# One bank per role: how five PSUM banks are handed out in the key/value stage of a linear-attention layer

## The chip, the cores and the metric

The kernel runs on one core of a Trainium2 chip. Its time is the device time in microseconds (us) of one execution, and the figure to compare is the median over several runs. The core has five engines with instruction streams of their own that run side by side and wait for each other through semaphores: TensorE (PE in the profile: matmuls, with weight loads shown as PEld), VectorE (DVE), ScalarE (ACT), GpSimd (POOL) and SyncE (SP), which starts the DMAs. Each engine executes its stream in order. Matmul results land in PSUM, which is divided into eight banks; a bank holds one 128 x 512 tile of f32. The other engines read the results from there.

## The reference, cut to what matters

The input x has 2048 rows of 1024. Four layers follow each other: attention, feed-forward, attention, feed-forward, with the same weights for both attention layers and for both feed-forward layers. Each adds to x.

```python
def _A_ref(x, wqkv, wo):          # x: layernorm of the running x
    qkv = (x @ wqkv) ...          # q, k, v: 32 heads of 32
    phi = lambda t: where(t > 0, t + 1, exp(t)) + 1e-6
    pq, pk = phi(q), phi(k)
    kv = einsum("bhsd,bhse->bhde", pk, v)
    z = einsum("bhsd->bhd", pk)
    num = einsum("bhqd,bhde->bhqe", pq, kv)
    den = einsum("bhqd,bhd->bhq", pq, z) + 1e-6
    return (num / den) ... @ wo

def _B_ref(x, w_gate, w_up, w_down):
    return ((x @ w_gate) * (x @ w_up)) @ w_down
```

The part that matters here is in the second attention layer: k = x @ wk and v = x @ wv for all 2048 rows, phi(k), and the sums kv and z over the rows.

## The kernel before, in words

The order of all work is written out by hand: the program emits the instructions engine by engine in the order in which the Python code runs, and the framework adds the semaphore waits that the data and the reuse of buffers need. Three queues hand out buffers, first in, first out (class `Free`): `slots` (SBUF, 8 KB a partition), `temps` (SBUF tiles of 128 x 512 f32) and `banks` (the eight PSUM banks). `get` takes the one that was returned longest ago; `put` returns one. A bank may be returned in the program while its last reader has yet to run: the next matmul that writes it then gets a wait for that reader.

The second attention layer computes k and v with a scheme of seven block products in place of eight (`kv_seven`). The contraction of 1024 is split in two halves, and so are the rows and the columns; sums and differences of blocks of x and of the weights are made ahead on VectorE (`x_sum`, `w_sum`). The stage has eight units (`unit(u)`). A unit makes k and v of two tiles of 128 rows, in 14 steps given by `SEQ` (L519). A step is one block product: four matmuls of 128 x 128 by 512 columns (L582), and then whatever the other engines do with the result. Step "6v" is product 6 for v.

Three of the eight banks hold the running sums kv and z (`kvp`) through the stage, so exactly five are left, and a unit uses five, in these roles:

- "ak" and "av": products 1, 6, 7 and 4 of k and of v, added onto each other;
- "ck" and "cv": products 5 and 3 of k and of v;
- "b": product 2, first of k, then of v. For k, ScalarE copies product 1 into it (L587) and 2k is added on top.

On its way the unit runs: ScalarE copies of partial results to SBUF (L558, L592), VectorE adds that bring a partial result and a bank together (L561, L566), the exponential of phi (L287) and its two VectorE passes (L291, L293). Work that is to be emitted a step or more later is put into `plan` by `later`: `out4` (L569), a ScalarE copy that reads the result of 4v out of "av", is emitted two steps after 4v, which is behind step 1k of the next unit. Behind 3k comes the exponential of a tile of 128 x 1024 (the "wide" one), its two VectorE passes one step later, and behind 3v the VectorE add L561 that reads "cv". After its steps a unit runs `kp` for the rows of the unit before it: 16 small matmuls (L527) that add into `kvp`.

The same plan holds work of other kinds: the layer norm of the rows of the second half (L234, L237, L242, L243, L245, L251, L258, L260, L262), their transposes by DMA (L274), the sums of x blocks (L218), loads of weights, and on GpSimd the cast of the query weights (L183).

A bank is taken when its role first occurs in a unit and returned when the program has emitted its last reader. In the order of the steps the roles take banks as ak and b (at 1k), ck (5k), av (1v), cv (5v). They return them as ak (4k), b (2v), ck (3k), cv (3v), and av last, since `out4` is emitted in the next unit. In the next unit the queue therefore gives ak, b and ck the banks that had the same role, gives av (at 1v) the bank of the old cv, and gives cv (at 5v) the bank of the old av.

The layer before ends with a product whose four banks are read by four VectorE instructions (L1167) and returned in that order; the stage's five banks are the last ones in the queue then. After the stage the queue goes on with the query projection (`q_step`, L791), which takes banks from it one by one.

Of the kernel before, what the change touches and what calls it, by code (L numbers as in the profile page):

```python
# [35 lines left out]
def kernel(  # L36
# [47 lines left out]
    banks = Free([psum.tile([P, NB], F32, tag=f"b{i}", name=f"b{i}") for i in range(8)])  # L84

    def v3(s, n):
        return s[:].rearrange("p (k n) -> p k n", n=n)
# [7 lines left out]
    def load_cols(view, n, parts=1):  # L95
        s = slots.get()
        w = KD // parts
        for r in range(parts):
            nc.sync.dma_start(out=v3(s, NB)[:, r * w:(r + 1) * w, :],
                              in_=view[:, r * w:(r + 1) * w, n * NB:(n + 1) * NB])  # L100
        return s
# [101 lines left out]
    def w_rhs(which, i):  # L203
        a11, a12, s4, a22, c, s3 = w_blocks(which)
        return {1: a11, 2: a12, 3: s4, 4: a22, 5: c[:, 0:KH], 6: c[:, KH:KD], 7: s3}[i]

    def x_blocks(g):
        x = h3(xnTs[(2, g)], NB)
        t = h3(xgs[g], 2 * P).rearrange("p (s k) n -> p s k n", k=KH)
        return x[:, 0:KH, 0:2 * P], x[:, KH:KD, 0:2 * P], x[:, 0:KH, 2 * P:NB], x[:, KH:KD, 2 * P:NB], t  # L210
# [73 lines left out]
    def phi_exp(b, c):  # L284
        m = temps.get()
        e = m[:].bitcast(BF16)[:, 0:b.shape[-1]]
        nc.scalar.activation(out=e, in_=b, func=ACT.Exp, bias=lns2[:, c:c + 1], scale=kaps[:, c:c + 1])  # L287
        return m, e
# [202 lines left out]
    def kv_seven(kvp):  # L491
        plan = {}

        def at(step, f, *args):
            plan.setdefault(step, []).append((f, args))

        for t, i in zip(range(2 * TPG, NT), (3, 8, 17, 31, 36, 45, 59, 64)):
            at(i, ln_stats, 2, t, (0,))
            if i % 14 == 8:
                at(i + 5, ln_norm, 2, t)  # L500
                at(i + 6, tr_tile, 2, t)
            else:
                at(i + 4, ln_rstd, 2, t)
                at(i + 6, ln_apply, 2, t)
                at(i + 7, tr_tile, 2, t)
        at(66, lambda: temps.put(st8.pop()))
        for g, i in ((1, 19), (2, 45), (3, 75)):
            for j in range(4):
                at(i + 2 * j, x_sum, g, j)
        at(8, load_w, "q", 0)  # L510
        at(9, load_w, "q", 1)
        for n in range(DC):
            for i in range(4):
                at(20 + 16 * n + 4 * i, cast_q, n, i)
        at(90, lambda: wA.update(o=[load_cols(wo_v, 0)]))

        pks = slots.get()
        pkv = v3(pks, D)
        SEQ = "1k 5k 1v 6k 2k 6v 7k 5v 7v 4k 2v 3k 4v 3v"  # L519
        wides = slots.get()  # L520
        wide = wides[:].bitcast(F32).rearrange("p (u n) -> p u n", n=D)

        def kp(t, first, last):
            u = t // TPG * 2 + t % 2
            r = 2 * (u % 2) + t % TPG // 2
            for c in range(KD):
                nc.tensor.matmul(out=kvp[c // 3][:, (c % 3) * VW:(c % 3) * VW + VW],  # L527
                                 lhsT=pkv[:, r, c * P:(c + 1) * P], rhs=vbs[r][:, c, :],
                                 start=first and c % 3 == 0, stop=last, skip_group_check=True)

        def tiles(u):
            return u // 2 * TPG + u % 2, u // 2 * TPG + u % 2 + 2

        def unit(u):
            g, pr = divmod(u, 2)
            b11, b21, b12, b22, t = x_blocks(g)
            lhs = {1: b11, 2: b21, 3: b22, 4: t[:, 3], 5: t[:, 0], 6: t[:, 1], 7: t[:, 2]}
            bk = {}
            tm = {}
            r0 = 2 * (u % 2)  # L540

            def pk(i, n):
                return pkv[:, r0 + i, n * NB:(n + 1) * NB]

            def vb(i, n):
                return vbs[r0 + i][:, n * (NB // P):(n + 1) * (NB // P), 0:P]

            def w4(a):
                return a[:].rearrange("p (c f) -> p c f", f=P)

            wd2 = wide[:, u % 2]

            def later(n, f, *args):
                at(u * 14 + j + n, f, *args)

            def copy(key, b):
                tm[key] = temps.get()
                nc.scalar.copy(out=tm[key][:], in_=b[:])  # L558

            def add(out, key, b):  # L560
                nc.vector.tensor_tensor(out=out, in0=w4(tm[key]), in1=w4(b), op=ALU.add)  # L561
                temps.put(tm.pop(key))

            def addw(n, b):
                v = wd2[:, n * NB:(n + 1) * NB]
                nc.vector.tensor_tensor(out=v, in0=v, in1=b[:], op=ALU.add)  # L566

            def out4(b):
                nc.scalar.copy(out=vb(0, 1), in_=w4(b))  # L569
                banks.put(b)  # L570

            for j, step in enumerate(SEQ.split()):
                i, w = int(step[0]), step[1]
                key = "b" if i == 2 else ("c" if i in (3, 5) else "a") + w
                if key not in bk:
                    bk[key] = banks.get()
                if i == 1 and w == "k":
                    bk["b"] = banks.get()
                b = bk[key]
                rhs = w_rhs(w, i)  # L580
                for k in range(KH):
                    nc.tensor.matmul(out=b[:], lhsT=lhs[i][:, k, pr * P:(pr + 1) * P], rhs=rhs[:, k, :],  # L582
                                     start=k == 0 and (i in (1, 5) or i == 2 and w == "v"), stop=k == KH - 1,
                                     skip_group_check=True)
                if i == 1:
                    if w == "k":
                        nc.scalar.copy(out=bk["b"][:], in_=b[:])  # L587
                    else:
                        copy("1v", b)
                elif i in (6, 7) and w == "k":  # L590
                    n = i - 6
                    nc.scalar.copy(out=wd2[:, n * NB:(n + 1) * NB], in_=b[:])  # L592
                    if i == 7:
                        later(1, addw, 1, bk["ck"])
                elif i == 6:
                    copy("6v", b)
                elif i == 7:
                    copy("7v", b)
                    add(vb(1, 1), "7v", bk["cv"])
                elif i == 3:  # L600
                    if w == "k":
                        addw(0, b)
                        later(1, phi_end, wd2, pkv[:, r0 + 1, :], 0, *phi_exp(wd2, 0))
                    else:
                        add(vb(1, 0), "6v", b)
                    banks.put(bk.pop(key))
                elif i == 2:
                    if w == "k":
                        phi_end(b[:], pk(0, 0), 0, *phi_exp(b[:], 0))
                    else:  # L610
                        add(vb(0, 0), "1v", b)
                        banks.put(bk.pop("b"))
                elif i == 4:
                    if w == "k":
                        phi_end(b[:], pk(0, 1), 0, *phi_exp(b[:], 0))
                        banks.put(bk.pop(key))
                    else:
                        later(2, out4, bk.pop(key))
                for f, args in plan.pop(u * 14 + j, ()):
                    f(*args)  # L620

        for u in range(2 * NG):
            unit(u)
            if u > 0:
                for t in tiles(u - 1):
                    kp(t, u == 1 and t == 0, False)
            if u % 2 == 1:
                slots.put(xgs.pop(u // 2))

        for i in sorted(plan):  # L630
            for f, args in plan[i]:
                f(*args)
        slots.put(*wA.pop("k"), *wA.pop("v"), wS.pop("k"), wS.pop("v"), wS.pop("d"), wides)
        wA["o"].append(load_cols(wo_v, 1))

        def rest():
            for t in tiles(2 * NG - 1):
                kp(t, False, t == NT - 1)
            slots.put(pks)
        return rest  # L640
# [92 lines left out]
    def layer_A(li, ahead):  # L733
        kvp = [banks.get() for _ in range(3)]
        rest = kv_eight(li, kvp) if li == 0 else kv_seven(kvp)

        kvx = slots.get()
# [551 lines left out]
```

## Time and profile before

| | us |
|---|---|
| median of 3 runs | 1510.17 |
| lowest and highest run | 1508.72 and 1510.45 |
| the profiled execution | 1509.88 |
| its span, first to last instruction | 1508.1 |
| the stage: first and last start of L582 | 757.7 and 872.9 |

The profile is one execution. Times in it are us from the start of its span. A timeline row gives the start, the duration, the engine and line, the operation with what it writes and reads and the shapes, and in brackets the idle time of the engine before it with the instruction that ended the wait. Rows of one line that follow each other are merged ("x8" is eight instructions). A matmul of 512 columns is shown with 379 ns, but matmuls overlap: they start about 216 ns apart when the clock is granted in full, so the shown end of a row is some 0.16 us behind the time at which the next matmul could start.

### The profile page before, as it was taken

How to read it: one execution, taken by the hardware profiler on the slowest of the kernel's cores; microseconds unless marked ns; L12 is line 12 of the kernel's file. 1: busy time of each engine (PE TensorE's matmuls, PEld its weight loads, DVE VectorE, ACT ScalarE, POOL GpSimd, SP SyncE). 2: the span in 40 equal slices, each digit the busy share in tenths (PEclk: the TensorE clock that was granted, in tenths of full speed). 3: DMA queues.
4: the chain of work that ended last, by engine and by line, in shares of the span. 5: the costliest groups of instructions: out<-in, count | busy, mean ns of one | idle time of the engine just before them, and what ended most of it. 6: DMA issues, size and time to landing. Idle time of an engine off the chain costs nothing.

```text
span 1508.1 us, 18371 instructions
## 1 busy us (share of the span) xinstructions
PE 1490.2 (99%) x7075; PEld 683.7 (45%) x7109; DVE 987.1 (65%) x1659; ACT 803.8 (53%) x1177; POOL 112.3 (7%) x54
## 2 busy tenths in 40 slices
PE   9999999999999999999989999999999999999999
PEld 4444444444444444444444444444444444444444
DVE  6666989988676666667966586854444854444452
ACT  4678875776667577665346575623335223333420
POOL 0000004972000000000050000000000000000000
PEclk9999999999999999999999999999999999999999
DMA  8696137464489788749431100564233678243513
GB/s 244 181 303 221 57 91 210 141 200 140 130 235 311 247 257 262 259 166 282 147 84 22 42 29 7 147 237 168 112 116 125 175 260 336 112 168 112 203 65 129
DMA packets 219655, 253.90 MB, mean 168 GB/s; under 512 B 68528, under 2 KB 195504, under 8 KB 208816
## 3 DMA queue, kind: packets, MB, share of 16 engines
q1 hardware_dynamic: 219568, 252.74, 52.7%
q8 instruction: 55, 0.90, 0.2%
q14 instruction: 32, 0.26, 0.1%
HBM read 196.08 MB, written 40.89 MB: 157 GB/s over the span
## 4 chain that ended last, share of the span: by engine, by line
PE 94%; DVE 4%; ACT 1%; DMA 1%; issue 1%; SPq 0%; DVEq 0%
PE b L954 45%; PE b L1194 22%; PE b L791 7%; PE b L654 7%; PE b L822 7%; PE b L582 4%; ACT f L287 1%; PE b L805 1%; DVE vb L561 1%; DVE s L293 1%; DVE f L291 1%; DMA s<-in_A_wqkv_dram 1%; PE b L673 1%; PE b L772 0%; DVE s L566 0%
## 5 line engine op out<-in xcount | busy, mean ns | idle before, releaser
L954 PE MATMUL b<-s,s 128*128 128x512 f16 x3136 | 677.7, 379 | 0.0
L954 PEld LDWEIGHTS <-s 128*128 128x128 f16 x3136 | 306.8, 98 | 369.8
L1194 PE MATMUL b<-s,s 128*128 128x512 f16 x1568 | 339.1, 379 | 0.0
L970 DVE TENSOR_TENSOR f<-f,b 128x512 f32<-128x512 f32 x232 | 159.3, 687 | 223.7 <-ACT f L959 209.5
L959 ACT COPY f<-b 128x512 f32<-128x512 f32 x284 | 166.2, 585 | 224.8 <-PE b L954 224.8
L1194 PEld LDWEIGHTS <-s 128*128 128x128 f16 x1568 | 153.4, 98 | 185.0
L965 ACT COPY b<-b 128x512 f32<-128x512 f32 x104 | 59.3, 570 | 128.3 <-PE b L954 128.3
L444 ACT ACTIVATE s<-s,scw 128x1024 f16<-128x1024 bf16 x112 | 122.8, 1151 | 2.0 <-DMA s<-in_B_w_gate_dram 1.8
L791 PE MATMUL b<-s,s 128*128 128x512 bf16 (+1 forms) x508 | 119.9, 379 | 0.2
L822 PE MATMUL b<-s,s 128*128 128x512 bf16 x495 | 117.5, 379 | 1.1 <-DVE s L814 0.3
L920 ACT ACTIVATE s<-s,scw 128x1792 f16<-128x1792 bf16 x48 | 83.0, 1784 | 61.5 <-DMA s<-in_B_w_down_dram 61.5
L654 PE MATMUL b<-s,s 128*128 128x512 bf16 x500 | 111.2, 379 | 1.1 <-DMA s<-in_A_wqkv_dram 0.3
L582 PE MATMUL b<-s,s 128*128 128x512 f16 x448 | 100.7, 383 | 10.1 <-DVE vb L561 10.1
L875 POOL TENSOR_SCALAR s<-s,scw 128x1024 f16<-128x1024 bf16 x28 | 88.0, 3160 | 256.8 <-DVE X L824 243.5
L974 DVE SCALAR_TENSOR_TENSOR s<-f,b 128x512 f16<-128x512 f32 x108 | 74.3, 688 | 40.5 <-PE b L954 24.2
L974 DVE SCALAR_TENSOR_TENSOR s<-f,f 128x512 f16<-128x512 f32 x116 | 83.2, 717 | 4.5 <-DVE f L970 0.5
L822 PEld LDWEIGHTS <-s 128*128 128x128 bf16 x512 | 50.0, 98 | 60.9 <-DVE s L814 1.0
L791 PEld LDWEIGHTS <-s 128*128 128x128 bf16 (+1 forms) x512 | 49.9, 98 | 59.5
L654 PEld LDWEIGHTS <-s 128*128 128x128 bf16 x512 | 49.7, 98 | 60.0 <-ACT s L280 1.0
L234 DVE BATCH_NORM_STATS2 st<-X 128x6 f32<-128x512 bf16 x112 | 71.7, 681 | 2.2 <-DMA X<-in_A_x_dram 2.2
L582 PEld LDWEIGHTS <-s 128*128 128x128 f16 x448 | 43.9, 99 | 64.0 <-issue 14.4
L1102 DVE TENSOR_TENSOR s<-s,s 128x1024 f16<-128x1024 f16 x80 | 52.9, 678 | 23.4 <-PE b L1194 23.4
(123 smaller groups left out, 1112.0 us busy)
## 6 DMA issues: line engine op xcount, KB each, us to landing
s<-wc SPq DMA_DIRECT2D x56, 1024.0 KB, 6.6
s<-dc SPq DMA_DIRECT2D x32, 896.0 KB, 5.5
wc<-s SPq DMA_DIRECT2D x28, 1024.0 KB, 5.0
s<-in_B_w_down_dram SPq DMA_DIRECT2D x24, 896.0 KB, 5.7
s<-in_A_wqkv_dram SPq DMA_DIRECT2D x17, 1024.0 KB, 7.9
s<-in_B_w_down_dram SPq DMA_DIRECT2D x14, 1024.0 KB, 8.3
s<-in_B_w_gate_dram SPq DMA_DIRECT2D x28, 512.0 KB, 6.7
s<-in_B_w_up_dram SPq DMA_DIRECT2D x28, 512.0 KB, 7.8
```

The lines of the kernel that those rows point to most:

```text
L444: nc.scalar.activation(out=h, in_=v, func=ACT.Copy, scale=scw[:, m:m + 1])
L582: nc.tensor.matmul(out=b[:], lhsT=lhs[i][:, k, pr * P:(pr + 1) * P], rhs=rhs[:, k, :], start=k == 0 and (i in (1, 5) or i == 2 and w == "v ...
L654: nc.tensor.matmul(out=b[:], lhsT=xnT[:, k, tl * P:(tl + 1) * P], rhs=w[:, k, :], start=(k == 0), stop=(k == KD - 1))
L791: nc.tensor.matmul(out=b[:], lhsT=w[:, k, j * P:(j + 1) * P], rhs=xnT[:, k, :], start=(k == 0), stop=(k == KD - 1))
L822: nc.tensor.matmul(out=b[:], lhsT=v3(pqs[g], G)[:, c, tl * P:(tl + 1) * P], rhs=v3(M[n], NB)[:, c, :], start=(c == 0), stop=(c == KD - 1))
L875: nc.gpsimd.tensor_scalar(out=h3(s, D)[:, i, :], in0=v3(s, D)[:, i, :], scalar1=scw[:, 2:3], scalar2=None, op0=ALU.mult)
L920: nc.scalar.activation(out=v.bitcast(F16)[:, r * w:(r + 1) * w], in_=v[:, r * w:(r + 1) * w], func=ACT.Copy, scale=scw[:, 2:3])
L954: nc.tensor.matmul(out=o[m][:], lhsT=W.get(j, m, st[i - 1], k), rhs=mv[i - 1][:, k, :], start=start and k == 0, stop=stop and k == KH - 1, ...
L959: nc.scalar.copy(out=d[m][:], in_=o[m][:])
L970: nc.vector.tensor_tensor(out=d[m][:], in0=d[m][:], in1=o[m][:], op=ALU.add)
L974: nc.vector.scalar_tensor_tensor(out=h3(hs[h], 2 * G)[:, pos, g * G:(g + 1) * G], in0=x[:], scalar=HS, in1=y[:], op0=ALU.mult, op1=ALU.mult)
L1194: nc.tensor.matmul(out=bank[(key, tl)][:], lhsT=lhs(i, j, tl), rhs=h3(wd[2 * pi + j // WPC], NB)[:, j % WPC, :], start=(j == 0 and i in (1 ...
```

## The change: what it does

The five banks are taken from the queue once, ahead of the units, and each keeps its role through all eight units; they go back to the queue together behind the stage. The gets and puts inside the units are gone. av then uses at 1v the bank that av had in the unit before, and cv at 5v the one that cv had. The order of the five gets is now ak, av, ck, cv, b, so in the first unit the roles meet other banks of the queue than before: only ak and ck meet the same ones. The order in which the five return at the end is ak, av, ck, cv, b; before, it was ak, b, ck, cv, av. The line numbers behind the deleted lines are lower by up to seven.

```diff
         SEQ = "1k 5k 1v 6k 2k 6v 7k 5v 7v 4k 2v 3k 4v 3v"
+        bk = {key: banks.get() for key in ("ak", "av", "ck", "cv", "b")}
         wides = slots.get()
...
-            bk = {}
             tm = {}
...
             def out4(b):
                 nc.scalar.copy(out=vb(0, 1), in_=w4(b))
-                banks.put(b)
 
             for j, step in enumerate(SEQ.split()):
                 i, w = int(step[0]), step[1]
                 key = "b" if i == 2 else ("c" if i in (3, 5) else "a") + w
-                if key not in bk:
-                    bk[key] = banks.get()
-                if i == 1 and w == "k":
-                    bk["b"] = banks.get()
                 b = bk[key]
...
                     else:
                         add(vb(1, 0), "6v", b)
-                    banks.put(bk.pop(key))
                 elif i == 2:
                     if w == "k":
                         phi_end(b[:], pk(0, 0), 0, *phi_exp(b[:], 0))
                     else:
                         add(vb(0, 0), "1v", b)
-                        banks.put(bk.pop("b"))
                 elif i == 4:
                     if w == "k":
                         phi_end(b[:], pk(0, 1), 0, *phi_exp(b[:], 0))
-                        banks.put(bk.pop(key))
                     else:
-                        later(2, out4, bk.pop(key))
+                        later(2, out4, b)
...
         slots.put(*wA.pop("k"), *wA.pop("v"), wS.pop("k"), wS.pop("v"), wS.pop("d"), wides)
+        banks.put(*bk.values())
```

## The prediction

> **What bounds the kernel now.** I read the busy shares of the page first, then the waits of TensorE, then the timeline of the stage that is changed, one unit boundary at a time.
>
> ```profile
> PE 1490.2 (99%) x7075; PEld 683.7 (45%) x7109; DVE 987.1 (65%) x1659; ACT 803.8 (53%) x1177; POOL 112.3 (7%) x54
> PE b L582 <- DVE vb L561: 10.1, 7, 2.5
> PE b L527 <- DVE vb L561: 0.4, 1, 0.4
> ```
>
> TensorE is busy 99% of the span, so the kernel can only get shorter where TensorE waits or runs slow. The two rows of waits are all that TensorE has between 750 and 900 us: its matmuls of the changed stage (L582) waited seven times, 10.1 us in total, for the VectorE add L561. Eight units have seven boundaries, so it is one wait a boundary. The timeline of the boundary from unit 2 to unit 3 shows which matmul waits, and behind what:
>
> ```profile
> 802.06 1.89 PE L582 MATMUL b<-s,s 128*128 128x512 f16 x8
> 805.12 10.52 PE L582 MATMUL b<-s,s 128*128 128x512 f16 x48 [1.17 <-DVE vb L561]
> ...
> 801.39 1.24 ACT L287 ACTIVATE f<-s,lns,kaps 128x1024 bf16<-128x1024 f32 x1 [1.62 <-DVE s L566]
> 802.53 0.28 ACT L258 ACTIVATE rstd<-mv,eps 128x1 f32<-128x1 f32 x1
> 802.85 0.20 ACT L260 ACTIVATE rstd<-rstd 128x1 f32<-128x1 f32 x1
> 803.12 0.57 ACT L587 COPY b<-b 128x512 f32<-128x512 f32 x1
> 803.60 0.59 ACT L569 CAST vb<-b 128x512 bf16<-128x512 f32 x1
> ...
> 802.66 0.55 DVE L291 TENSOR_SCALAR f<-f,scw,epss 128x1024 bf16<-128x1024 bf16 x1 [1.31 <-ACT f L287]
> 803.24 1.23 DVE L293 SCALAR_TENSOR_TENSOR s<-s,f 128x1024 bf16<-128x1024 f32 x1
> 804.38 0.68 DVE L561 TENSOR_TENSOR vb<-f,b 128x512 bf16<-128x512 f32 x1
> ...
> 805.08 0.04 issue
> ```
>
> The columns are start, duration, engine, line, operation, and in brackets the idle time before it; the last row is of the chain of waits. Eight matmuls are 1k and 5k of unit 3; the 48 after them begin with 1v. 1v is held until 805.12, and the add before it ends at 804.38 + 0.68 = 805.06: that is step 3v of unit 2, the last VectorE work on the old unit, queued behind the wide exponential (801.39) and two VectorE passes over its result. It holds 1v because 1v took from the queue the bank that 3v had just returned.
>
> **The change, part by part.** The code issues the same instructions in the same order on every engine; only bank numbers and the waits that follow from them differ. No instruction, DMA or queue position moves, so I cost only waits.
>
> *1v.* Its bank is now the one of 4v, whose last reader is the ScalarE cast L569, issued right behind the copy L587 of 1k. In the rows the cast ends at 803.60 + 0.59 = 804.19. From a releasing instruction's end to 1v the chain has 0.04 us (the issue step), so 1v could have started at 804.23 in place of 805.12: 0.89 us gained. The same reading at the other six boundaries, a cast and the held 1v each:
>
> ```profile
> 772.53 0.58 ACT L569 CAST vb<-b 128x512 bf16<-128x512 f32 x1
> 774.48 3.44 PE L582 MATMUL b<-s,s 128*128 128x512 f16 x8 [2.48 <-DVE vb L561]
> 788.88 0.59 ACT L569 CAST vb<-b 128x512 bf16<-128x512 f32 x1
> 790.76 3.61 PE L582 MATMUL b<-s,s 128*128 128x512 f16 x16 [1.53 <-DVE vb L561]
> 817.97 0.59 ACT L569 CAST vb<-b 128x512 bf16<-128x512 f32 x1
> 819.74 1.46 PE L582 MATMUL b<-s,s 128*128 128x512 f16 x6 [1.43 <-DVE vb L561]
> 832.59 0.59 ACT L569 CAST vb<-b 128x512 bf16<-128x512 f32 x1
> 834.11 2.10 PE L582 MATMUL b<-s,s 128*128 128x512 f16 x9 [1.17 <-DVE vb L561]
> 846.95 0.59 ACT L569 CAST vb<-b 128x512 bf16<-128x512 f32 x1
> 848.73 2.54 PE L582 MATMUL b<-s,s 128*128 128x512 f16 x11 [1.43 <-DVE vb L561]
> 861.58 0.59 ACT L569 CAST vb<-b 128x512 bf16<-128x512 f32 x1
> 862.75 2.53 PE L582 MATMUL b<-s,s 128*128 128x512 f16 x11 [0.83 <-DVE vb L561]
> ```
>
> With the same 0.04 us the gains are 1.33, 1.25, 1.14, 0.89, 1.15 and 0.54 us; with the 0.89 above, 7.19 us. What is late next is the cast itself: about 10.1 - 7.2 = 2.9 us of waiting stays, 1.15 at the first boundary (there the wide exponential reaches the copy late) and 0.28 at the others.
>
> *The slow clock behind the longest wait.* The first boundary's 2.48 us is followed by slow matmuls:
>
> ```profile
> 772.01:774.48 2.47, 0.00 (x1) 0.00 (x0) 0.95 0.00 0
> 774.48:777.66 3.18, 3.18 (x8) 1.17 (x8) 0.50 0.35 67
> 777.66:790.76 13.10, 10.78 (x50) 4.65 (x48) 1.00 0.13 24
> 790.76:805.12 14.36, 12.41 (x56) 5.43 (x56) 1.00 0.10 19
> ```
>
> These are stretches of the stage (start and end, length, TensorE busy, weight loads, then the granted clock). For 3.18 us after the wait the clock was granted at 0.50: eight matmuls in that time, half the usual number. The 1.53 us and shorter waits of the other boundaries are followed by 1.00. In the changed kernel the longest is 1.15 us, so I expect no slow stretch, and 3.18 x 0.50 = 1.59 us come back. The other end is nothing. [...]
>
> *5v.* It now takes the bank of the old 3v. It starts five steps of four matmuls behind 1v: (10.52 - 0.38) / 47 = 0.216 us a matmul, so 4.3 us later, at about 808.5 for unit 3, where the add has ended at 805.06. Cost nothing; if the add came over 3.5 us later it would wait.
>
> *1k's copy in unit 0.* The five banks come out of the queue in the order in which the stage before returned them, and the order of the five gets is another one. The bank that 1k's copy seeds for 2k is now the last of four that the last VectorE reads of the layer before return, not the first:
>
> ```profile
> 757.42 2.73 DVE L1167 SCALAR_TENSOR_TENSOR X<-b,kap,X 128x512 bf16<-128x512 f32 x4 [3.25 <-PE b L1194]
> 758.89 12.83 PEld L582 LDWEIGHTS <-s 128*128 128x128 f16 x60 [0.27 <-issue]
> 758.93 0.57 ACT L587 COPY b<-b 128x512 f32<-128x512 f32 x1 [9.51 <-PE b L582]
> ```
>
> The copy can start at 757.42 + 2.73 = 760.15 instead of 758.93 and ends at about 760.74. 5k starts at 758.89, so 6k, which overwrites what the copy reads, eight matmuls later at 760.61: it waits about 0.2 us. The copy of 1v, next on ScalarE, needs 1v's end, after 760.7 too, and is not touched. Cost 0.2 us.
>
> *VectorE in unit 1.* Here GpSimd still runs, and VectorE's tensor-scalar passes are longer beside it:
>
> ```profile
> 759.86 22.62 POOL L183 TENSOR_SCALAR s<-s,scw 128x1024 f16<-128x1024 bf16 x8 [412.59 <-DMA s<-in_A_wqkv_dram]
> 779.64 1.26 DVE L291 TENSOR_SCALAR f<-f,scw,epss 128x512 bf16<-128x512 bf16 x1 [3.40 <-ACT f L287]
> 784.06 0.41 DVE L291 TENSOR_SCALAR f<-f,scw,epss 128x512 bf16<-128x512 bf16 x1
> 787.02 1.24 ACT L287 ACTIVATE f<-s,lns,kaps 128x1024 bf16<-128x1024 f32 x1 [1.98 <-DVE s L566]
> 788.40 0.57 ACT L587 COPY b<-b 128x512 f32<-128x512 f32 x1
> ```
>
> GpSimd ends at 782.48. Unit 1 runs some 3 us earlier after the change, so the pass of 784.06 comes to about 781.3, beside GpSimd, and may take up to 1.26 - 0.41 = 0.85 us longer. All behind it on VectorE, the wide exponential (787.02) with it, moves by that, and the slack before the copy is 788.40 - 788.26 = 0.14. So 0 to 0.7 us are lost; I take 0.4, in the middle, as the passes beside GpSimd vary.
>
> *VectorE at the other boundaries.* 1v is now ahead of VectorE by up to 1.15 us more. In unit 3 VectorE still has its norm work and one sum to do:
>
> ```profile
> 806.29 0.68 DVE L218 TENSOR_TENSOR s<-s 128x1024 f16<-128x1024 f16 x1
> 808.72 0.41 DVE L291 TENSOR_SCALAR f<-f,scw,epss 128x512 bf16<-128x512 bf16 x1 [1.76 <-ACT f L287]
> ```
>
> It then idles 1.76 us, more than the 0.89 us that unit 3 moves against it. Cost nothing.
>
> *Behind the stage.* The five banks go back in another order; the projections that take them next start after their last readers in both orders, and TensorE's remaining waits there are 0.4 us (L527, above), so I let the gain pass through unchanged.
>
> The sum: 7.19 + 1.59 - 0.2 - 0.4 = 8.2 us. The profiled execution took 1509.88 us with a span of 1508.1, so the forecast is 1501.7, 0.5% less. That execution stands 0.3 us below the median of 1510.17; the runs shown lie 1.7 us apart (1508.72 to 1510.45), about the size of one slow-clock stretch, so runs without it may exist.
>
> **The rivals.**
>
> *The slow stretch stays.* Its place is not the wait's doing, and a half-clock stretch of 1.59 us is met in unit 1 at any rate. [...] Against it: in the whole stage it stands only behind the longest wait. 1509.88 - (8.2 - 1.6) = 1503.3. [...]
>
> *The wait moves on.* TensorE runs ahead by 1 us a unit and meets VectorE at another step, 5v or 7v, so that the total wait is as before. It decides if VectorE falls 3.5 us behind 1v. Against it: VectorE's idle time before the first exponential of a unit (1.76 above, 3.40 in unit 1). Only the slow stretch would come back: about 1508.3 to 1509.9, within the measurement.
>
> *ScalarE becomes the bound.* 1v now stands behind a ScalarE queue: wide exponential, two short ones, copy, cast. From the exponential's end (802.63) the old path took 805.12 - 802.63 = 2.49 us, the new one 804.23 - 802.63 = 1.60. If the exponential itself, with whatever is ahead of it, came 2 us later against TensorE, each boundary would lose 2 - 0.9 = 1.1 us, 7.7 in all: 1517.6, slower. It decides at 0.9 us of delay a boundary. For it: the queue is in order, and the copy starts within 0.1 us of the end of the short ones. Against it: what delays the exponential delays the old path as well, and nothing is added to ScalarE.
>
> **How the numbers follow.** A difference under 0.2%, 3 us, is about what a measurement of this kernel cannot tell from no change. Forecast 0.74; the slow stretch stays 0.13; the wait moves on 0.08; ScalarE the bound 0.05. The first two are faster by over 3 us; of the third I count a little (0.01) as faster and the rest as same: faster 0.88, same 0.07, slower 0.05. The forecast's own range is its 0 to 0.7 of unit 1 and the spread of the runs: 1500.2 to 1502.5. The range to 1504.6 takes in the second case with 1.3 us for the runs.
>
> **What would show it.** (Lines as in the kernel before.) Right: TensorE's waits at this stage fall from 10.1 to about 2.9 us and name the ScalarE cast; the granted clock is 1.00 through unit 1; the start of unit 2's 1v comes near 787.2 instead of 790.76, that of unit 7 near 854.6 instead of 862.75; 6k of unit 0 shows a wait of 0.2 us. Wrong: waits under the adds L561 or the exponential L287 at other steps, a clock of 0.5 anywhere between 770 and 800 us, or a gain at the stage's end that the later stages do not keep.

## The result and the profile after

The changed kernel takes 1502.28 us (median of 6 runs, 1501.33 to 1503.61); the kernel before took 1510.31 in the same comparison (6 runs, 1508.72 to 1510.87). The ratio is 0.9948, with a 95% interval of 0.9935 to 0.9961: 8 us or 0.5% faster. About half of the runs of the kernel before have a mean granted clock of 0.999, like its profiled execution with the stretch of half clock, and the others 1.000 (the runs are counted under long_wait), so the gain is 8.1 us against the former and 6.5 us against the latter. The profiled execution took 1502.76 us with a span of 1501.0.

The busy shares of the page, and TensorE's waits between 750 and 900 us (the line waiting and the one waited for, us in total, times, the longest):

```profile
PE 1488.1 (99%) x7075; PEld 683.3 (46%) x7109; DVE 988.4 (66%) x1659; ACT 803.9 (54%) x1177; POOL 114.1 (8%) x54
PE b L577 <- ACT vb L569: 3.5, 7, 1.7
PE b L528 <- DVE vb L561: 0.4, 1, 0.4
```

L577 is the old L582, the matmul of the units. It waits seven times as before, but for the ScalarE cast of 4v (L569) instead of the VectorE add of 3v, and for 3.5 us instead of 10.1. The boundary from unit 2 to unit 3 in the timeline of the changed kernel:

```profile
799.51 1.89 PE L577 MATMUL b<-s,s 128*128 128x512 f16 x8
801.70 1.67 PE L577 MATMUL b<-s,s 128*128 128x512 f16 x7 [0.30 <-ACT vb L569]
...
798.83 1.24 ACT L287 ACTIVATE f<-s,lns,kaps 128x1024 bf16<-128x1024 f32 x1 [1.61 <-DVE s L566]
800.57 0.57 ACT L582 COPY b<-b 128x512 f32<-128x512 f32 x1
801.05 0.59 ACT L569 CAST vb<-b 128x512 bf16<-128x512 f32 x1
801.83 0.68 DVE L561 TENSOR_TENSOR vb<-f,b 128x512 bf16<-128x512 f32 x1
```

The exponential, the copy of 1k (now L582) and the cast stand where they stood against 1k and 5k. But 1v begins at 801.70, 0.06 us behind the cast's end (801.64), while the add that held it before ends only at 802.51.

The same matmuls in stretches from one 1v to the next (start and end, length, TensorE busy, weight loads, granted clock):

```profile
758.50:774.72 16.22, 14.45 (x65) 6.25 (x65) 1.00 0.36 104
774.72:788.21 13.49, 12.41 (x57) 5.44 (x57) 1.00 0.21 39
788.21:801.70 13.49, 12.41 (x57) 5.44 (x57) 1.00 0.11 21
...
842.17:855.66 13.49, 12.41 (x57) 5.41 (x56) 1.00 0.05 18
```

From unit 1 on each unit takes 13.49 us, and the clock is granted in full. Before, by the starts of 1v that the prediction shows, they took 16.28, 14.36, 14.62, 14.37, 14.62 and 14.02. Unit 0 with the first boundary takes 16.22 instead of 16.61. Together 7.72 us are gained between 1k of unit 0 and 1v of unit 7. The span is 7.1 us shorter and not 7.7, because in this execution the stage began 0.6 us later (758.50 instead of 757.87). Behind the stage TensorE has the same wait of 0.4 us and no new one: the later stages keep the gain.

### The profile page after: what moved, and what is told of

Its sections match the earlier page's. It is cut to its first block, busy times and chain, and to the rows that moved or that the text cites. A ratio compares the mean times of both kernels' runs of the same rounds, so it can differ in the third digit from the quotient of the medians.

```text
span 1501.0 us, 18364 instructions
## 1 busy us (share of the span) xinstructions
PE 1488.1 (99%) x7075; PEld 683.3 (46%) x7109; DVE 988.4 (66%) x1659; ACT 803.9 (54%) x1177; POOL 114.1 (8%) x54
## 4 chain that ended last, share of the span: by engine, by line
PE 96%; DVE 2%; ACT 1%; DMA 1%; issue 0%; SPq 0%; DVEq 0%; ACTq 0%
PE b L947 45%; PE b L1187 23%; PE b L784 7%; PE b L647 7%; PE b L815 7%; PE b L577 5%; PE b L798 1%; DMA s<-in_A_wqkv_dram 1%; PE b L666 1%; PE b L765 0%; PE b L528 0%; ACT b L582 0%; ACT vb L569 0%; DVE st L234 0%; DVE X L1160 0%
## 5 line engine op out<-in xcount | busy, mean ns | idle before, releaser
L577 PE MATMUL b<-s,s 128*128 128x512 f16 x448 | 99.4, 379 | 3.6 <-ACT vb L569 3.5
L577 PEld LDWEIGHTS <-s 128*128 128x128 f16 x448 | 43.5, 98 | 56.7 <-issue 6.4
```

## The experiments

All are edits of the changed kernel, but for one that says so. Each ratio is against runs of the kernel before on the same chip, which had a median of 1509.11 us (25 runs) beside the first four runs, 1509.93 (14 runs) beside the next four and 1510.15 (8 runs) beside the last two.

| run | median, us | ratio to the kernel before, 95% interval |
|---|---|---|
| swap_all | 1513.37 | 1.0019 (1.0009 to 1.0028) |
| swap_first | 1507.41 | 0.9984 (0.9975 to 0.9994) |
| swap_rest | 1508.00 | 0.9991 (0.9982 to 1.0001) |
| first_order | 1501.63 | 0.9949 (0.9935 to 0.9964) |
| cast_at_4v | 1498.73 | 0.9928 (0.9914 to 0.9942) |
| cast_before_exp | 1498.01 | 0.9925 (0.9912 to 0.9938) |
| gpsimd_late | 1502.61 | 0.9953 (0.9939 to 0.9967) |
| long_wait | 1507.51 | 0.9985 (0.9976 to 0.9994) |
| queue_cast_4v | 1497.57 | 0.9921 (0.9907 to 0.9936) |
| best | 1497.61 | 0.9920 (0.9907 to 0.9933) |

### The exchange of av and cv: swap_all, swap_rest, swap_first

The first lines of a unit put the exchange back that the queue made; the condition is `u > 0`, `u > 1` or `u == 1`:

```diff
         def unit(u):
+            if u > 0:
+                bk["av"], bk["cv"] = bk["cv"], bk["av"]
             g, pr = divmod(u, 2)
```

> The five banks stay taken through the stage, as in the changed kernel, but av and cv exchange their banks at the start of every unit from unit 1 on, as the queue did. Theory (the exchange alone costs the time): 1v waits seven times for the VectorE add of 3v, 10 to 13 us in all, a stretch of granted clock 0.5 follows the longest wait, and the time is that of the kernel before plus the 0.3 us of the first unit: about 1510.6. Rival (it is the fixed roles as such, the order of the first gets or the order in which the banks go on to the query projection): the time stays near 1502.3.

> As the changed kernel, but av and cv exchange their banks at the start of units 2 to 7 and not of unit 1. Theory: the first boundary waits 1.2 to 1.7 us for the ScalarE cast, the six others for the VectorE add as before (1.53, 1.17, 1.43, 1.17, 1.43, 0.83 us); no slow clock; slower than the changed kernel by 1.25 + 0.89 + 1.14 + 0.89 + 1.15 + 0.54 = 5.9 us: 1508.1. Rival (the slow stretch stands in unit 1 whatever the first wait is, or waits of 1.5 us also make it): a stretch of 0.5 is seen, about 1509.7.

> As the changed kernel, but av and cv exchange their banks once, at the start of unit 1. Theory (the long wait makes the clock fall): the first boundary's wait grows from 1.7 to between 2.5 and 4.4 us (it now ends with the VectorE add), the others stay at 0.3; behind it the granted clock is 0.5 for some 3.4 us, which costs 1.6 us; in all 2.4 to 4.3 us more than the changed kernel, about 1505.5. Rival (the slow stretch is not the wait's doing): granted clock 1.00 through unit 1, and only 0.8 to 2.7 us more, about 1504.

TensorE's waits in the three, in this order (two lines are inserted, so the matmul is L579, the add L563, the cast L571):

```profile
PE b L579 <- DVE vb L563: 11.9, 7, 4.4
```

```profile
PE b L579 <- DVE vb L563: 7.6, 6, 1.6
PE b L579 <- ACT vb L571: 1.1, 1, 1.1
```

```profile
PE b L579 <- DVE vb L563: 2.4, 1, 2.4
PE b L579 <- ACT vb L571: 1.8, 6, 0.3
```

Each boundary waits for VectorE exactly where the banks are exchanged. With all seven exchanged the whole gain is lost, and more; so it is this exchange whose removal gave the gain, and not the fixed roles as such. swap_rest came out at 1508.0, for 1508.1 expected. swap_all is 4 us above the kernel before and 2.8 above what was expected: in its profiled execution the first wait is 4.4 us instead of 2.5, as three VectorE passes ahead of the add took 1.23, 1.46 and 2.02 us (0.43, 0.85 and 1.23 in the kernel before, with GpSimd running in both), and the half-clock stretch at it is of double length (6.83 us for 3.41). Each run also has a mean granted clock, to three places. The two runs of swap_all with 1.000 took 1508.68 and 1509.77 us, close to the 1508.09 to 1509.59 of the kernel before at 1.000; the eight longer ones have 0.999 or 0.998.

swap_first is the odd one. Its profiled execution took 1503.67 us, with a wait of 2.42 us and a granted clock of 1.00 behind it; its other nine runs took 1504.98 to 1508.31, and all nine have a mean granted clock of 0.999 or 0.998. Their median puts swap_first 1.9 us above the 1505.5 expected. So a wait of 2.42 us was not followed by the slow clock here, while one of 2.48 us was in the kernel before.

### The slow clock behind a wait: long_wait

```diff
         def unit(u):
+            if u == 4:
+                bk["av"], bk["cv"] = bk["cv"], bk["av"]
...
                     else:
+                        if u == 3:
+                            pad = temps.get()
+                            for r in range(4):
+                                nc.vector.bn_stats(out=pad[:][:, 8 * r:8 * r + 6], in_=X[:, r, 0:NB])
+                            temps.put(pad)
                         add(vb(1, 0), "6v", b)
```

> As the changed kernel, but av and cv exchange their banks once, at the start of unit 4, and four VectorE passes of 0.6 us without use stand ahead of unit 3's add of 3v. So one wait of 1.43 + 2.4 = 3.8 us is made at a boundary where GpSimd is idle. Theory (a long enough wait lets the clock fall, wherever it is): granted clock 1.00 in unit 1 and 0.5 for 3.4 us or more behind this wait; slower than the changed kernel by 3.5 us of waiting and 1.7 us or more of half clock: 1507.5. Rival (the slow stretch belongs to unit 1): no stretch behind this wait, 1505.8.

The median is 1507.51. The profile has one wait of 3.8 us at unit 4, and behind it the slow clock; unit 1, behind a wait of 1.1 us, has none (its 48 matmuls took 10.52 us, and 12.07 in the kernel before):

```profile
PE b L579 <- DVE vb L563: 3.8, 1, 3.8
...
818.26:821.25 2.99, 2.99 (x8) 1.03 (x8) 0.50 0.00 0
821.25:833.22 11.97, 10.89 (x51) 4.75 (x50) 1.00 0.12 24
```

The slow clock stands behind the wait and not in unit 1. The record of the granted clock also shows when it changes: it is 0.50 from 774.25 to 777.66 us in the kernel before (3.41 us), from 775.12 to 781.95 in swap_all (6.83 us) and from 817.84 to 821.25 in long_wait (3.41 us). These are the 3.41 us ahead of each fall, with TensorE's busy time in them (the second figure). First the kernel before, then swap_all with the first half of its slow stretch as second row, then long_wait:

```profile
770.84:774.25 3.41, 1.16 (x6) 0.41 (x5) 2.50 (x3) 2.23 (x5) 3.41 (x3) 1.00 0.14 25
```

```profile
771.71:775.12 3.41, 1.02 (x4) 0.38 (x4) 2.11 (x2) 2.62 (x5) 3.41 (x2) 1.00 0.01 1
775.12:778.53 3.41, 1.39 (x4) 0.54 (x4) 3.23 (x5) 0.00 (x0) 3.41 (x2) 0.50 0.00 0
```

```profile
814.43:817.84 3.41, 0.04 (x1) 0.00 (x0) 3.41 (x6) 0.29 (x1) 0.00 (x0) 1.00 0.00 0
```

Ahead of these falls TensorE was busy for 1.16, 1.02 and 0.04 us of the 3.41. The wait of swap_first, and the matmuls behind it, at a clock of 1.00 throughout:

```profile
773.22:775.64 2.42, 0.01 (x1) 0.00 (x0) 1.00 0.00 0
775.64:779.05 3.41, 3.41 (x16) 1.56 (x16) 1.00 0.40 75
```

So in the profiled executions half clock came with the waits of 2.48, 3.8 and 4.4 us, and not with those of 2.42 us and of 1.67 us (the longest of the changed kernel). What sets 2.42 and 2.48 us apart is not shown.

The granted clock also accounts for the times of the kernel before. Its 25 runs beside the first four fall into 15 from 1508.30 to 1509.30 and 10 from 1510.23 to 1510.65; the middles (1508.73 and 1510.36) are 1.6 us apart. The mean granted clock of each run tells the two apart: it is 1.000 in all 15 and 0.999 in all 10, and one stretch of 3.41 us at 0.50 would bring the mean of 1508 us to 0.9989. Over all 47 runs beside the experiments it is 1.000 in the 24 from 1508.09 to 1509.59 and 0.999 in the 23 from 1509.80 to 1510.70. That the loss in each of these 23 stands behind the first boundary is not shown, since the place of a stretch is known for the profiled executions alone.

### The first unit: first_order and gpsimd_late

```diff
-        bk = {key: banks.get() for key in ("ak", "av", "ck", "cv", "b")}
+        bk = {key: banks.get() for key in ("ak", "b", "ck", "av", "cv")}
```

> As the changed kernel, but the five banks are taken in the order ak, b, ck, av, cv, that of the kernel before. Theory: in unit 0 the copy of 1k no longer waits for the last VectorE read of the layer before, 6k does not wait, and the 64 matmuls of unit 0 and the first two steps of unit 1 take 14.1 us instead of 14.5. The time falls by 0.2 to 0.4 us, too little for the times to show: 1502.0. Rival (the order of the first gets matters more, or the other way): the time differs by over 1 us from 1502.3.

```diff
-        at(8, load_w, "q", 0)
-        at(9, load_w, "q", 1)
+        at(66, load_w, "q", 0)
+        at(67, load_w, "q", 1)
...
-                at(20 + 16 * n + 4 * i, cast_q, n, i)
+                at(68 + 8 * n + 2 * i, cast_q, n, i)
```

> As the changed kernel, but the query weights are loaded and cast on GpSimd from about unit 5 on instead of from unit 0 on. Theory (the first boundary is late because VectorE's passes are longer beside GpSimd): the first boundary waits 0.3 us as the others do, VectorE's pass ahead of the wide exponential takes 0.4 us there instead of 1.1, and the longer passes turn up in units 5 to 7; the stage is 1.0 to 1.4 us shorter if those are hidden: 1501. Rival (the first unit is late for a reason of its own, its first banks or the norm work): the first boundary stays at 1.1 to 1.7 us.

The changed kernel's unit 0 in the timeline:

```profile
758.50 14.54 PE L577 MATMUL b<-s,s 128*128 128x512 f16 x64
761.50 1.39 PEld L577 LDWEIGHTS <-s 128*128 128x128 f16 x7 [0.37 <-issue]
760.88 0.57 ACT L582 COPY b<-b 128x512 f32<-128x512 f32 x1 [10.82 <-DVE X L1160]
...
768.95 1.10 DVE L291 TENSOR_SCALAR f<-f,scw,epss 128x512 bf16<-128x512 bf16 x1
772.00 1.24 ACT L287 ACTIVATE f<-s,lns,kaps 128x1024 bf16<-128x1024 f32 x1 [2.36 <-DVE s L566]
773.28 1.46 DVE L291 TENSOR_SCALAR f<-f,scw,epss 128x1024 bf16<-128x1024 bf16 x1 [1.31 <-ACT f L287]
774.77 2.02 DVE L293 SCALAR_TENSOR_TENSOR s<-s,f 128x1024 bf16<-128x1024 f32 x1
```

and first_order's:

```profile
758.39 14.13 PE L577 MATMUL b<-s,s 128*128 128x512 f16 x64
759.45 0.57 ACT L582 COPY b<-b 128x512 f32<-128x512 f32 x1 [9.52 <-PE b L577]
```

As predicted, 1k's copy waits for the last VectorE read of the layer before (L1160 here), and 6k starts at 761.50, at the copy's end. With the old order the copy waits for its matmuls alone, and the 64 matmuls take 14.13 us instead of 14.54. The times cannot show 0.4 us: 1501.63 against 1502.28.

gpsimd_late tells how much of the long first wait is GpSimd's doing. Its waits, and VectorE's passes at the first boundary and beside GpSimd in unit 5:

```profile
774.06 10.52 PE L577 MATMUL b<-s,s 128*128 128x512 f16 x48 [1.10 <-ACT vb L569]
769.02 0.36 DVE L291 TENSOR_SCALAR f<-f,scw,epss 128x512 bf16<-128x512 bf16 x1
...
836.44 2.75 PE L577 MATMUL b<-s,s 128*128 128x512 f16 x12 [0.48 <-DVE s L566]
842.33 10.52 PE L577 MATMUL b<-s,s 128*128 128x512 f16 x48 [0.47 <-ACT vb L569]
842.21 2.01 DVE L293 SCALAR_TENSOR_TENSOR s<-s,f 128x1024 bf16<-128x1024 f32 x1
```

The longer passes moved with GpSimd, as the theory has it: at the first boundary the pass takes 0.36 us, and the 2.0 us pass of 128 x 1024 turns up at 842. But the first wait fell only to 1.10 us and not to 0.3. With GpSimd in its old place it was 1.67 us in the changed kernel, 1.3 in first_order, 1.1 in swap_rest and in long_wait; and in swap_first the same pass took only 0.36 us beside GpSimd. So GpSimd adds between nothing and 0.6 us, and that is all that the theory holds for. The rest is there without GpSimd. What differs at the first boundary is that unit 0 has no unit before it and so no `kp`: the 16 small matmuls of L528, which hold TensorE for 0.95 us between 3v and 1k at every other boundary, are missing. The wait for the same ScalarE work is longer by about that much (1.10 against 0.30). That is worked out from the code and the rows; no run added matmuls there. The move gained nothing (1502.61 us), since GpSimd's new place has waits of its own.

### The wait that is left: cast_at_4v, cast_before_exp, queue_cast_4v, best

```diff
-                        later(2, out4, b)
+                        out4(b)
```

> As the changed kernel, but the ScalarE cast that reads 4v out of av is emitted right behind 4v, one unit boundary earlier, behind the wide exponential and ahead of 1k's copy. Theory (what holds 1v now is the cast behind 1k's copy): 1v does not wait at the clean boundaries, 0.46 us less at each of six by the starts of the matmuls; at the first boundary about 0.7 us stay, since the cast is still behind the wide exponential there. In all some 3.5 us: 1498.5. Rival (1k's copy, now later on ScalarE, holds 6k instead): a new wait of 6k for the copy of about the size of the one removed, no gain.

cast_before_exp has this edit and puts the wide exponential into the plan, behind the cast:

```diff
-                        later(1, phi_end, wd2, pkv[:, r0 + 1, :], 0, *phi_exp(wd2, 0))
+                        later(1, lambda: phi_end(wd2, pkv[:, r0 + 1, :], 0, *phi_exp(wd2, 0)))
```

> As cast_at_4v, and the wide exponential of phi is emitted behind the cast instead of ahead of it. Theory: 4v ends before the exponential can start, so the exponential loses nothing, and the cast is done long before 1v; no wait at any boundary but the first, where 6k waits about 0.5 us for 1k's copy: 1498.2. Rival (the exponential is pushed back and with it 1k's copy): waits of 6k at the other boundaries, no better than cast_at_4v.

TensorE's waits in cast_at_4v, and its ScalarE timeline at the boundary to unit 3:

```profile
PE b L577 <- ACT vb L569: 0.7, 1, 0.7
PE b L577 <- DVE s L566: 0.2, 1, 0.2
```

```profile
797.40 1.24 ACT L287 ACTIVATE f<-s,lns,kaps 128x1024 bf16<-128x1024 f32 x1 [1.62 <-DVE s L566]
798.55 0.56 ACT L569 CAST vb<-b 128x512 bf16<-128x512 f32 x1
799.45 0.58 ACT L582 COPY b<-b 128x512 f32<-128x512 f32 x1
```

The same two views of cast_before_exp:

```profile
PE b L577 <- DVE s L566: 0.4, 1, 0.4
PE b L577 <- ACT b L582: 0.3, 1, 0.3
```

```profile
797.04 0.59 ACT L569 CAST vb<-b 128x512 bf16<-128x512 f32 x1 [0.68 <-PE b L577]
797.97 1.24 ACT L287 ACTIVATE f<-s,lns,kaps 128x1024 bf16<-128x1024 f32 x1 [0.34 <-DVE s L566]
```

In both no wait is left at six of the seven boundaries. The cast is done ahead of 1k's copy, and at these six the copy does not hold 6k; it does in unit 1 of cast_before_exp, for 0.3 us (about 0.5 was expected). cast_at_4v gains 3.5 us as expected (1498.73 for 1498.5). cast_before_exp loses the first boundary's 0.7 us wait and has two short ones in its place; 1498.01 against 1498.73 is within the spread of the runs (1497.29 to 1499.57).

queue_cast_4v is the kernel before, queue and all, with one line changed; best is cast_before_exp with first_order's order of gets:

```diff
-                        later(2, out4, bk.pop(key))
+                        out4(bk.pop(key))
```

> The kernel before, with its queue, and only the ScalarE cast of 4v moved: emitted right behind 4v, so that av's bank goes back ahead of cv's. Theory (what matters is whose last reader a step inherits, not that the roles are fixed): the queue then hands every role its own bank again, the waits under the VectorE add of 3v vanish, and the time is that of cast_at_4v less the 0.3 us of the first unit: 1498.4. Rival (taking the banks once is what helps): waits for the VectorE add remain and the time stays above 1502.

> cast_before_exp together with the get order of first_order. Theory: the first unit's 0.3 us and the rest add up, no wait over 0.5 us in the stage: 1497.8, within the noise of cast_before_exp. Rival (they share one wait of 6k at the start): no difference from cast_before_exp, 1498.0.

The kernel before with nothing but the earlier cast has no wait of the unit matmuls left in the view of waits, and in the timeline the 112 matmuls of units 0 and 1 stand in one row:

```profile
PE b L527 <- DVE vb L561: 0.4, 1, 0.4
```

```profile
757.82 24.84 PE L582 MATMUL b<-s,s 128*128 128x512 f16 x112
```

At 0.216 us from start to start the 112 matmuls would take 24.4 us, so 0.5 us of delays are in the row that are too short to show as waits; 0.3 of them are at 1v of unit 1. At 1497.57 us the run is faster than the changed kernel, and the same as best (1497.61) within the runs. The queue works as well as fixed roles, once the banks go back in the order in which the next unit takes them. Both ways beat both kernels, by 12.5 us against the kernel before (1510.15).

## Why the prediction was right

The forecast was 1501.7 us; 1502.28 was measured, and the profiled execution took 1502.76, against the 1509.88 from which the sum was made. Step by step, in the profile, by the starts of 1v:

- *1v at boundaries two to seven*: predicted 1.25, 0.89, 1.14, 0.89, 1.15 and 0.54 us. Units 2 to 6 gained 0.87, 1.13, 0.88, 1.13 and 0.53: right to 0.02 each. What holds 1v is the cast, as said. swap_all and swap_rest show that the exchange of banks was the cause of the old waits, cast_at_4v that the cast is the cause of the new ones.
- *1v at the first boundary* was mis-sized: 1.33 predicted, and 1.1 for unit 0 as a whole after the 0.2 of 1k's copy, where 0.39 was measured. The wait there is 1.67 us instead of 1.15. The sum took the place of the wide exponential from one execution; with GpSimd running, VectorE's pass ahead of it took 1.10 us this time and 0.43 then.
- *The slow clock*: right for this pair of executions; the clock is 1.00 through unit 1, and in long_wait 0.50 follows a wait of 3.8 us in another unit. The rival in which the slow stretch stays did not come about. The prediction noted that runs without a stretch may exist, and by their mean clock of 1.000 about half of the runs of the kernel before are such: for them the 1.59 us are no gain. That the measured medians lie 8 us apart, like the sum, is in part luck, as four of the six runs of the kernel before in that comparison took over 1510 us, like the runs elsewhere with a mean clock of 0.999; against the 25 runs with a median of 1509.11 the gain would be 6.8.
- *VectorE in unit 1*: 0.4 us of loss predicted, none found: GpSimd ran until 783.9, but the passes of 128 x 512 in unit 1 took 0.36 and 0.41 us, and the unit takes 13.49 us like those without GpSimd, a gain of 2.79 (2.44 predicted: 1.25 + 1.59 - 0.4).
- *1k's copy in unit 0*: 0.2 us predicted; 0.25 at 6k, and another 0.17 at 5k of unit 1, which waited for a VectorE add made late by the same GpSimd passes. first_order is 0.41 shorter over both.
- *5v*, *VectorE elsewhere*, *behind the stage*: nothing predicted and nothing seen.

The errors of the first two units (0.74 too much, 0.35 too little) and some hundredths leave 7.72 of 8.2; that these two errors have opposite signs is luck too. The rival in which the wait moves on is excluded by the rows of waits. The one with ScalarE as the bound has its mechanism right (ScalarE is what holds 1v now) and its price wrong, since at six of the seven boundaries nothing delays the exponential; at the first, where it came later, the wait was 0.5 us longer than in the sum.

## What to carry to other kernels

A buffer that is taken from a queue ties a step to the last reader of whatever came back before it. Look in the waits for a matmul that is released by an instruction of another product, and then either keep a role on its buffer or, better here, let the last reader run earlier so that the buffers return in the order of use: one moved line gave 12.5 us, where the fixed roles gave 8. A wait on the path can have a second price: here half clock came with waits of 2.48, 3.8 and 4.4 us (with one of 2.42 us it did not), so the longest of several can be worth more than its length.

## What the runs showed of the hardware that was not expected

With one wait of 2.48 us (the kernel before) came a half-clock stretch of 3.41 us, with one of 2.42 (the profiled execution of swap_first) none. In the 3.41 us ahead of the fall TensorE was busy for 1.16 us in the kernel before and for 1.02 in swap_all.

Beside GpSimd's scaling passes some VectorE passes took longer and others did not. In the changed kernel the pass over 128 x 1024 with an f32 operand in SBUF (L293) took 2.02 us instead of 1.23, in the kernel before 1.23 although GpSimd ran then too; the tensor-scalar pass over 128 x 1024 (L291) took 0.85 in the kernel before, swap_first and gpsimd_late and 1.46 in the changed kernel and swap_all, instead of 0.55. The adds with a PSUM operand (L561, L566) kept their 0.68 in the changed kernel.
